# A dense layer with Mish on one core: the first block grows from 256 to 512 rows, half of it loaded by a DMA transpose that goes third on its queue

## The chip, the core and the metric

The kernel runs on one core of a Trainium2 chip. A core has a matrix engine (TensorE, PE in the profile, whose weight loads are shown as PEld), a vector engine (DVE), a scalar engine (ACT), GpSimd (POOL) and a queue engine (SP) that here only issues transfers. The engines run by themselves and meet at semaphores. Matrix products land in PSUM, eight banks of 128 partitions by 512 float32 values; everything else lies in SBUF, with 128 partitions too. The metric is the device time of one execution in microseconds.

## The reference

```python
def reference(x, w1, b1, w2):
    h = jnp.einsum("bsd,df->bsf", x, w1) + b1
    sp = jnp.log1p(jnp.exp(-jnp.abs(h))) + jnp.where(h > 0, h, jnp.zeros_like(h))
    act = h * jnp.tanh(sp)
    return jnp.einsum("bsf,fd->bsd", act, w2)
```

All tensors are bfloat16: x is 1 x 2048 x 512, w1 is 512 x 1792, b1 has 1792 values, w2 is 1792 x 512. So there are two matrix products with the Mish function between them.

## The kernel before

The 2048 rows of x are cut into blocks of 256, 512, 512, 512 and 256 rows (`BLOCKS`), and a block into tiles of 128 rows. For each block the kernel first computes the hidden layer, 14 slices `f` of 128 hidden units: `mm1_step` multiplies one 128 x 128 piece of w1 (slice f, one of four pieces k of the inner dimension) with the block's rows of x, which must lie transposed in `xT`, so four matmuls as wide as the block make one slice in one PSUM bank. ACT then adds b1 and applies Mish in one instruction per slice (`mish`), from PSUM into `a_sb`. After the 14 slices, `mm2` computes the output: for each tile of 128 rows, 14 matmuls of 512 columns accumulate over f in one bank, DVE copies the bank to `o_sb`, and SP stores it (`put`). The last tile is cut into 384 and 128 columns so that its second store is small.

The order is the order in which the code is written; there is no scheduler. Each engine waits only where `wait` puts a semaphore, and a `Stream` leaves out waits that an earlier one already covers.

The start is special. x must be transposed before it can be multiplied. For the first block, SP loads its two tiles as they are (`x_nat`), PE transposes them through PSUM in eight 128 x 128 transposes (`transpose_x`), and DVE and ACT copy one half of each tile to `xT`. For all later blocks SP issues DMA transposes that write `xT` straight from memory. SP issues in this order: tiles 0 and 1 of x, w1 for slices 4 to 7 (512 KB), w1 for slices 8 to 13 (768 KB), w2 for slices 0 to 4 (640 KB), w2 for slices 5 to 13 (1152 KB), and then the four DMA transposes. ACT issues w1 for slices 0 to 3 in two halves of 256 KB (k = 0, 1 and k = 2, 3), and b1. While the first transfers are under way, PE runs six matmuls of 512 columns on constants (`WARM`, `dummy`) that nobody reads. The first block's slices 0 to 3 are multiplied tile by tile as the copies land, and its second product runs f by f over both tiles at once, so that each piece of w2 is used as it lands. b1 arrives as 14 rows and is turned into a column per slice by one more PE transpose and a DVE copy (`b1_sb`).

Of the kernel before, what the change touches and what calls it, by code (L numbers as in the profile page):

```python
# [4 lines left out]

P = 128
WARM = (512,) * 6
BLOCKS = (256, 512, 512, 512, 256)


class Stream:
# [20 lines left out]
def bass_standalone__dense_activation_mish__prompt_kernel(  # L32
# [20 lines left out]
    F0 = 4  # L53
    N0 = BLOCKS[0] // P

    with ExitStack() as es:
        def sb(name, shape, t):
            return es.enter_context(nc.sbuf_tensor(name, shape, t))

        x_nat = sb("x_nat", [P, N0, D], BF)  # L60
# [4 lines left out]
        b1_pad = sb("b1_pad", [P, P], BF)  # L65
# [10 lines left out]
        sp = Stream(nc.sync, None)  # L76
        pe = Stream(nc.tensor, sem("c_pe"))
# [4 lines left out]
        def load(q, dst, src, name, transpose=False):  # L82
            s = sem(name)
            (q.eng.dma_start_transpose if transpose else q.eng.dma_start)(dst, src).then_inc(s, 16)  # L84
            return (s, 16)

        def load_w1(q, ks, a, b):
            return load(q, w1_sb[:, ks, a * P:b * P], w1v[:, ks, a * P:b * P], "s_w1_%d_%d" % (ks.start, a))


        t_xn, t_w1, t_w2 = [None] * N0, {}, {}
        for ks in (slice(0, 2), slice(2, 4)):
            t = load_w1(act, ks, 0, F0)
            for f in range(F0):
                for k in range(ks.start, ks.stop):
                    t_w1[k, f] = t
        for j in range(N0):
            t_xn[j] = load(sp, x_nat[:, j, :], x2[j * P:(j + 1) * P, :], "s_xn%d" % j)
        t_b1 = load(act, b1_nat[:, :], b1.rearrange("(j p) -> j p", p=P), "s_b1")
        for a, b in ((4, 8), (8, FT)):  # L100
            t = load_w1(sp, slice(0, KT), a, b)
            for f in range(a, b):
                for k in range(KT):
                    t_w1[k, f] = t
        for a, b in ((0, 5), (5, FT)):
# [3 lines left out]
        t_xT = [None]  # L109
# [15 lines left out]
        def dummy(n):  # L125
            nc.tensor.matmul(ps[:, 7, 0:n], c_w, c_m[:, 0:n], start=True, stop=True)  # L126


        free = [[] for _ in range(8)]
        t_cp = {}  # L130
        t_mish = {}

        def transpose_x(j):

            pe.wait(t_xn[j], t_id)
            for h, eng in ((0, dve), (1, act)):
                bank = 2 * j + h
                psb = ps[:, bank, 0:P].bitcast(BF)
                for i in range(2):
                    k = 2 * h + i  # L140
                    mm = nc.tensor.transpose(psb[:, i * P:(i + 1) * P], x_nat[:, j, k * P:(k + 1) * P], ident[:, :])  # L141
                eng.wait(pe.mark(mm))
                dst = xT[:, 2 * h:2 * h + 2, j * P:(j + 1) * P]
                src = psb.rearrange("p (k t) -> p k t", k=2)
                t = eng.mark(nc.vector.tensor_copy(dst, src) if eng is dve else act.eng.activation(dst, src, ACT.Copy))  # L145
                t_cp[j, h] = t
                free[bank] = [t]

        def mish(s, f, bank, t_mm):
            n = BLOCKS[s]  # L150
            act.wait(t_b1c, t_mm)
            t = act.mark(act.eng.activation(a_sb[:, f, starts[s]:starts[s + 1]], ps[:, bank, 0:n], ACT.Mish,  # L152
                                            bias=b1_sb[:, f:f + 1]))
            t_mish[s, f] = t
            free[bank] = [t]

        def mm1_step(s, f, k, bank, js=None):

            n = BLOCKS[s]
            lo, hi = (0, n) if js is None else (js[0] * P, (js[-1] + 1) * P)  # L160
            first = k == 0 and lo == 0
            if first:
                pe.wait(*free[bank])
            pe.wait(t_w1[k, f])
            if s:
                pe.wait(t_xT[s])
            else:
                pe.wait(*[t_cp[j, k // 2] for j in (js or range(N0))])
            return nc.tensor.matmul(ps[:, bank, lo:hi], w1_sb[:, k, f * P:(f + 1) * P],  # L169
                                    xT[:, k, starts[s] + lo:starts[s] + hi], start=first, stop=(k == KT - 1))  # L170

        def mm1(s, f, bank):
            for k in range(KT):
                mm = mm1_step(s, f, k, bank)
            mish(s, f, bank, pe.mark(mm))

        s_out = sem("s_out")
        n_out = 0

        def mm2_step(i, f, lo, hi, bank):  # L180
            s = max(b for b in range(len(BLOCKS)) if starts[b] <= i * P)
            if f == 0:
                pe.wait(*free[bank])
            pe.wait(t_w2[f], t_mish[s, f])
            return nc.tensor.matmul(ps[:, bank, 0:hi - lo], a_sb[:, f, i * P:(i + 1) * P], w2_sb[:, f, lo:hi],  # L185
                                    start=(f == 0), stop=(f == FT - 1))

        def put(i, lo, hi, bank, t_mm):
            nonlocal n_out
            dve.wait(t_mm)  # L190
            t = dve.mark(nc.vector.tensor_copy(o_sb[:, i, lo:hi], ps[:, bank, 0:hi - lo]))  # L191
            free[bank] = [t]
            sp.wait(t)
            sp.eng.dma_start(out2[i * P:(i + 1) * P, lo:hi], o_sb[:, i, lo:hi]).then_inc(s_out, 16)
            n_out += 1

        def mm2(i, lo, hi, bank):
            for f in range(FT):
                mm = mm2_step(i, f, lo, hi, bank)
            put(i, lo, hi, bank, pe.mark(mm))  # L200
# [7 lines left out]
        t_b1p = dve.mark(nc.vector.tensor_copy(b1_pad[0:FT, :], b1_nat[:, :]))  # L208
        done = []
        for js, ks in (((0,), (0, 1)), ((1,), (0, 1)), ((0, 1), (2, 3))):  # L210
            for k in ks:
                for f in range(F0):
                    mm = mm1_step(0, f, k, 4 + f, js)
                    if k == KT - 1:
                        done.append((f, 4 + f, pe.mark(mm)))
        for k in range(KT):
            mm = mm1_step(0, F0, k, 1)
        done.append((F0, 1, pe.mark(mm)))
        pe.wait(t_b1p, *free[0])
        psb1 = ps[:, 0, 0:P // 2].bitcast(BF)  # L220
        t_b1t = pe.mark(nc.tensor.transpose(psb1, b1_pad[:, :], ident[:, :]))  # L221
        dve.wait(t_b1t)
        t_b1c = dve.mark(nc.vector.tensor_copy(b1_sb[:, :], psb1[:, 0:FT]))  # L223
        free[0] = [t_b1c]
        for f, bank, t in done:
            mish(0, f, bank, t)
        for f in range(F0 + 1, FT):
            mm1(0, f, {5: 2, 6: 3, 7: 0, 12: 2, 13: 3}.get(f, 4 + f % 4))
        for f in range(FT):
            for j in range(N0):  # L230
                mm = mm2_step(j, f, 0, D, j)
                if f == FT - 1:
                    put(j, 0, D, j, pe.mark(mm))

        for s in range(1, len(BLOCKS)):
            for f in range(FT):
                mm1(s, f, 4 + f % 4)
# [35 lines left out]
```

## Time and profile before

| what | value |
|---|---|
| median of 3 runs | 106.25 us (106.18 to 106.25) |
| the profiled execution's own time: its span, first to last instruction | 105.4 us |
| PE busy | 101.1 us (96%), 532 matmuls recorded |
| PE weight loads busy | 52.0 us |
| ACT busy | 42.3 us |
| DVE busy | 12.2 us |
| DMA moved | 7.94 MB |
| granted TensorE clock, mean | 1.000 |

The runs' median is 0.85 us above the profiled span, since a run's time also holds what lies around the first and the last instruction. A busy PE in such a table is not a PE at its best pace, since matmuls overlap and are recorded from entering to leaving: two kernels are compared by when each stage starts, not by busy time.

### The profile page before, as it was taken

What the parts mean: (1) busy time and instruction counts of PE and PEld (TensorE: products, weight loads), DVE (VectorE), ACT (ScalarE), POOL (GpSimd) and SP (SyncE); (2) the same over time, 40 slices, a digit from 0 to 9 for tenths busy, and PEclk for the clock granted to TensorE, in tenths of its full rate; (3) what the DMA queues carried; (4) which work ended last, traced back from release to release, by engine and by line L of the source; (5) the groups of instructions that cost most, each with busy time, mean ns of one, the idle gap of its engine ahead of it and who ended that gap; (6) DMA issues with size and microseconds to landing.
All of it is one profiled execution on the core that took longest, in us unless ns stands there. A gap on an engine that the chain in (4) does not pass through costs nothing.

```text
span 105.4 us, 1227 instructions
## 1 busy us (share of the span) xinstructions
PE 101.1 (96%) x532; PEld 52.0 (49%) x541; DVE 12.2 (12%) x22; ACT 42.3 (40%) x73; POOL 0.7 (1%) x6
## 2 busy tenths in 40 slices
PE   6889999999999999999999999999999999999992
PEld 2477734444444444444444444444444444688462
DVE  0200000400001122200000222200000222200023
ACT  0607910477770000277771000177772000199100
POOL 2000000000000000000000000000000000000000
DMA  1999999980000111000000110110000101110011
GB/s 45 361 364 358 346 207 146 255 214 0 0 0 0 50 53 53 24 25 0 3 0 0 50 50 14 42 50 0 0 0 0 49 5 45 50 56 0 0 50 50
DMA packets 13489, 7.94 MB, mean 75 GB/s; under 512 B 7852, under 2 KB 13484, under 8 KB 13484
## 3 DMA queue, kind: packets, MB, share of 16 engines
q1 hardware_dynamic: 12912, 7.34, 26.3%
q10 hardware_dynamic: 572, 0.53, 1.5%
q8 instruction: 4, 0.07, 0.3%
q14 instruction: 1, 0.01, 0.0%
HBM read 3.94 MB, written 2.10 MB: 57 GB/s over the span
## 4 chain that ended last, share of the span: by engine, by line
PE 84%; DMA 11%; SPq 2%; issue 1%; DVE 0%
PE ps L185 44%; PE ps L169 40%; DMA w_sb<-in_w_dram 11%; SPq L84 2%; DVE o_sb L191 0%
## 5 line engine op out<-in xcount | busy, mean ns | idle before, releaser
L152 ACT ACTIVATE a_sb<-ps,b_sb 128x512 bf16<-128x512 f32 (+1 forms) x70 | 40.2, 611 | 52.2 <-PE ps L169 49.3
L169 PE MATMUL ps<-xT,w_sb 128*128 128x512 bf16 (+2 forms) x285 | 50.0, 334 | 0.7 <-DMA w_sb<-in_w_dram 0.3
L185 PE MATMUL ps<-w_sb,a_sb 128*128 128x512 bf16 (+2 forms) x232 | 48.7, 366 | 0.4
L169 PEld LDWEIGHTS ps<-xT,w_sb 128*128 128x128 bf16 x288 | 27.8, 100 | 22.2 <-DMA w_sb<-in_w_dram 0.6
L185 PEld LDWEIGHTS ps<-w_sb,a_sb 128*128 128x128 bf16 x238 | 22.7, 98 | 25.8 <-DMA w_sb<-in_w_dram 0.6
L191 DVE CAST o_sb<-ps 128x512 bf16<-128x512 f32 (+2 forms) x17 | 11.1, 660 | 84.3 <-PE ps L185 84.3
L126 PE MATMUL ps<-const-bfloat16-1.0 128*128 128x512 bf16 x6 | 2.7, 623 | 0.8 <-PEq L258 0.8
L120 ACT ACT_TABLE_LOAD x1 | 1.3, 1283 | 2.5 <-issue 2.5
L126 PEld LDWEIGHTS ps<-const-bfloat16-1.0 128*128 128x128 bf16 x6 | 0.7, 133 | 1.9 <-issue 1.9
L141 PE MATMUL ps<-ident,x_nat 128*128 128x128 bf16 x8 | 1.2, 309 | 0.4 <-DMA x_nat<-in_x_dram 0.4
L141 PEld LDWEIGHTS ps<-ident,x_nat 128*128 128x128 bf16 x8 | 0.7, 134 | 1.4 <-DMA x_nat<-in_x_dram 1.4
L145 ACT ACTIVATE xT<-ps 128x256 bf16<-128x256 bf16 x2 | 0.8, 384 | 0.9 <-PE ps L141 0.9
L145 DVE COPY xT<-ps 128x256 bf16<-128x256 bf16 x2 | 0.6, 292 | 3.6 <-PE ps L141 3.6
L208 DVE COPY b_pad<-b_nat 14x128 bf16<-14x128 bf16 x1 | 0.2, 182 | 1.6 <-DMA b_nat<-in_b_dram 1.6
L223 DVE CAST b_sb<-ps 128x14 f32<-128x14 bf16 x1 | 0.2, 174 | 1.3 <-PE ps L221 1.3
L118 POOL TENSOR_SCALAR_AFFINE_SELECT ident<-ones 128x128 bf16<-128x128 bf16 x1 | 0.3, 294 | 0.1
L221 PE MATMUL ps<-ident,b_pad 128*128 128x128 bf16 x1 | 0.2, 219 | 0.0
L115 DVE MEMSET b_pad<- 128x64 uint32 x1 | 0.1, 112 | 0.9 <-PEq L258 0.9
L116 POOL MEMSET ones<- 128x128 bf16 x1 | 0.2, 205 | 0.3 <-POOLq L258 0.3
L221 PEld LDWEIGHTS ps<-ident,b_pad 128*128 128x128 bf16 x1 | 0.1, 98 | 0.0
L258 POOL MEMSET const-bfloat16-1.0<- 128x1 bf16 x1 | 0.1, 102 | 0.0
L258 POOL MEMSET const-uint8-127<- 128x1 uint8 x1 | 0.1, 102 | 0.0
(2 smaller groups left out, 0.2 us busy)
## 6 DMA issues: line engine op xcount, KB each, us to landing
out_dram<-o_sb SPq DMA_DIRECT2D x15, 128.0 KB, 1.7
w_sb<-in_w_dram SPq DMA_DIRECT2D x1, 1152.0 KB, 11.4
w_sb<-in_w_dram SPq DMA_DIRECT2D x1, 768.0 KB, 7.4
w_sb<-in_w_dram SPq DMA_DIRECT2D x1, 640.0 KB, 8.7
w_sb<-in_w_dram ACTq DMA_DIRECT2D x2, 256.0 KB, 3.5
w_sb<-in_w_dram SPq DMA_DIRECT2D x1, 512.0 KB, 5.8
x_nat<-in_x_dram SPq DMA_DIRECT2D x2, 128.0 KB, 2.8
out_dram<-o_sb SPq DMA_DIRECT2D x1, 96.0 KB, 1.6
```

The lines of the kernel that those rows point to most:

```text
L84: (q.eng.dma_start_transpose if transpose else q.eng.dma_start)(dst, src).then_inc(s, 16)
L116: t_ones = pool.mark(pool.eng.memset(ones[:, :], 1.0))
L118: t_id = pool.mark(pool.eng.affine_select(ident[:, :], ones[:, :], pattern=[[1, P]], compare_op=ALU.is_equal, fill=0.0, base=0, channel_mu ...
L120: act.eng.preload_act_table(ACT.Mish)
L126: nc.tensor.matmul(ps[:, 7, 0:n], c_w, c_m[:, 0:n], start=True, stop=True)
L141: mm = nc.tensor.transpose(psb[:, i * P:(i + 1) * P], x_nat[:, j, k * P:(k + 1) * P], ident[:, :])
L145: t = eng.mark(nc.vector.tensor_copy(dst, src) if eng is dve else act.eng.activation(dst, src, ACT.Copy))
L152: t = act.mark(act.eng.activation(a_sb[:, f, starts[s]:starts[s + 1]], ps[:, bank, 0:n], ACT.Mish, bias=b1_sb[:, f:f + 1]))
L169: return nc.tensor.matmul(ps[:, bank, lo:hi], w1_sb[:, k, f * P:(f + 1) * P], xT[:, k, starts[s] + lo:starts[s] + hi], start=first, stop=( ...
L185: return nc.tensor.matmul(ps[:, bank, 0:hi - lo], a_sb[:, f, i * P:(i + 1) * P], w2_sb[:, f, lo:hi], start=(f == 0), stop=(f == FT - 1))
L191: t = dve.mark(nc.vector.tensor_copy(o_sb[:, i, lo:hi], ps[:, bank, 0:hi - lo]))
L221: t_b1t = pe.mark(nc.tensor.transpose(psb1, b1_pad[:, :], ident[:, :]))
```

## The change

`BLOCKS` becomes four blocks of 512, so the first block now has tiles 0 to 3. Tiles 0 and 1 are loaded and transposed on PE as before. Tiles 2 and 3 come by a DMA transpose of 256 rows, which SP issues third, behind tiles 0 and 1 of x and ahead of all of w1 and w2 that SP loads. The other three DMA transposes, of 512 rows each, stay behind w2.

On PE the constants' matmuls are now five of 512 columns and three of 128, and two more of 128 columns stand behind the transposes of tile 0. Slices 0 to 3 are multiplied in this order: tile 0 with k = 0, the transposes of tile 1, tile 0 with k = 1, tile 1 with k = 0 and 1, both tiles with k = 2 and 3 (256 columns), and then tiles 2 and 3 slice by slice (256 columns). From slice 4 on every matmul of the first product has 512 columns. The second product of the first block runs tile by tile, as in the other blocks.

DVE alone copies the transposed x tiles (128, 384, 256 and 256 columns), and b1 is turned by four 32 x 32 transposes on DVE in place of the one on PE. The store of the last 128 columns is issued by ACT and no longer by SP.

```diff
-WARM = (512,) * 6
-BLOCKS = (256, 512, 512, 512, 256)
+WARM = (512,) * 5 + (128,) * 3
+GAP = (128,) * 2
+FIRST = ((0, 2), (2, 4))
+BLOCKS = (512, 512, 512, 512)
...
+        for ks in FIRST:
+            load_w1(act, slice(*ks), 0, F0)
+        load_x(0)
+        load_x(1)
+        t_b1 = load(act, b1_nat[:, :], b1.rearrange("(j p) -> j p", p=P), "s_b1")
+        load_xT(2 * P, 4 * P)
+        load_w1(sp, slice(0, KT), 4, 8)
+        load_w1(sp, slice(0, KT), 8, FT)
+        load_w2(0, 5)
+        load_w2(5, FT)
         for s in range(1, len(BLOCKS)):
-            lo, hi = starts[s], starts[s + 1]
-            t_xT.append(load(sp, xT[:, :, lo:hi], x2[lo:hi, :], "s_xT%d" % s, True))
+            load_xT(starts[s], starts[s + 1])
...
         for n in WARM:
             dummy(n)
-        transpose_x(0)
-        transpose_x(1)
+        transpose_x(0, 6, (0,))
+        transpose_x(0, 5, (1, 2, 3))
+        for n in GAP:
+            dummy(n)
+        for k in range(2):
+            for f in range(F0):
+                mm1_step(0, f, k, f, 0, 1)
+            if k == 0:
+                transpose_x(1, 6, (0, 1))
+                transpose_x(1, 4, (2, 3))
         dve.wait(t_b1, t_bz)
         t_b1p = dve.mark(nc.vector.tensor_copy(b1_pad[0:FT, :], b1_nat[:, :]))
...
+        for c in range(P // 32):
+            t_b1t = dve.mark(nc.vector.transpose(b1_t[c * 32:(c + 1) * 32, :], b1_pad[:, c * 32:(c + 1) * 32]))
...
+        for k in range(2):
+            for f in range(F0):
+                mm1_step(0, f, k, f, 1, 2)
+        for k in range(2, KT):
+            for f in range(F0):
+                mm1_step(0, f, k, f, 0, 2)
+        for f in range(F0):
+            for k in range(KT):
+                mm = mm1_step(0, f, k, f, 2, 4)
+            mish(0, f, f, pe.mark(mm))
...
-                    mm2(i, D - P, D, (i + 1) % 4)
+                    mm2(i, D - P, D, (i + 1) % 4, act)
```

The order of instructions on PE from the start to the end of the first block, before. L126 is the matmuls on constants, L141 the transposes of x, L169 the first product, L221 the transpose of b1, L185 the second product:

```order
L126 MATMUL ps<-const-bfloat16-1.0 128x512 x6
L141 MATMUL ps<-ident,x_nat 128x128 x8
L169 MATMUL ps<-xT,w_sb 128x128 x16
L169 MATMUL ps<-xT,w_sb 128x256 x12
L221 MATMUL ps<-ident,b_pad 128x128
L169 MATMUL ps<-xT,w_sb 128x256 x36
L185 MATMUL ps<-w_sb,a_sb 128x512 x28
```

The same stretch of PE after the change, where L134 is the constants, L145 the transposes, L163 the first and L191 the second product:

```order
L134 MATMUL ps<-const-bfloat16-1.0 128x512 x5
L134 MATMUL ps<-const-bfloat16-1.0 128x128 x3
L145 MATMUL ps<-ident,x_nat 128x128 x4
L134 MATMUL ps<-const-bfloat16-1.0 128x128 x2
L163 MATMUL ps<-xT,w_sb 128x128 x4
L145 MATMUL ps<-ident,x_nat 128x128 x4
L163 MATMUL ps<-xT,w_sb 128x128 x12
L163 MATMUL ps<-xT,w_sb 128x256 x24
L163 MATMUL ps<-xT,w_sb 128x512 x40
L191 MATMUL ps<-w_sb,a_sb 128x512 x56
```

Four multiplications of tile 0 moved ahead of the transposes of tile 1, and the block's narrow matmuls (256 columns) went from 48 to 24, with 40 of 512 columns behind them.

SP's loads before, in the order of issue (x_nat are tiles 0 and 1, the four w_sb rows are w1 for slices 4 to 7 and 8 to 13 and w2 for 0 to 4 and 5 to 13):

```order
L84 DMA x_nat<-in_x_dram 128x512 x2
L84 DMA w_sb<-in_w_dram 128x4x512
L84 DMA w_sb<-in_w_dram 128x4x768
L84 DMA w_sb<-in_w_dram 128x5x512
L84 DMA w_sb<-in_w_dram 128x9x512
L84 DMA_TRANSPOSE xT<-in_x_dram 128x4x512 x3
L84 DMA_TRANSPOSE xT<-in_x_dram 128x4x256
```

SP's loads after the change:

```order
L86 DMA x_nat<-in_x_dram 128x512 x2
L86 DMA_TRANSPOSE xT<-in_x_dram 128x4x256
L86 DMA w_sb<-in_w_dram 128x4x512
L86 DMA w_sb<-in_w_dram 128x4x768
L86 DMA w_sb<-in_w_dram 128x5x512
L86 DMA w_sb<-in_w_dram 128x9x512
L86 DMA_TRANSPOSE xT<-in_x_dram 128x4x512 x3
```

The DMA transpose of 256 rows moved from the end of the row of loads to its third place, ahead of four copies of weights.

More of the change, by code (lines that the diff above doesn't have):

```diff
@@ L58, in sb @@
             return es.enter_context(nc.sbuf_tensor(name, shape, t))
-        x_nat = sb("x_nat", [P, N0, D], BF)
+        x_nat = sb("x_nat", [P, 2, D], BF)
         xT = sb("xT", [P, KT, S], BF)
@@ L64, in bass_standalone__dense_activation_mish__prompt_kernel @@
         b1_nat = sb("b1_nat", [FT, P], BF)
[L65 removed]
+        b1_pad = sb("b1_pad", [32, P], BF)
+        b1_t = sb("b1_t", [P, 32], BF)
         b1_sb = sb("b1_sb", [P, FT], F32)
@@ L85, in load, with load_x, load_w2 @@
             return (s, 16)
+        t_xn, t_w1, t_w2, t_xT = [None] * 2, {}, {}, {}
+        def load_x(j):
+            t_xn[j] = load(sp, x_nat[:, j, :], x2[j * P:(j + 1) * P, :], "s_xn%d" % j)
         def load_w1(q, ks, a, b):
[L88 to L94, printed above, removed]
+            t = load(q, w1_sb[:, ks, a * P:b * P], w1v[:, ks, a * P:b * P], "s_w1_%d_%d" % (ks.start, a))
+            for f in range(a, b):
                 for k in range(ks.start, ks.stop):
                     t_w1[k, f] = t
[L97 to L105, printed above, removed]
+        def load_w2(a, b):
             t = load(sp, w2_sb[:, a:b, :], w2v[:, a:b, :], "s_w2_%d" % a)
@@ L131, in bass_standalone__dense_activation_mish__prompt_kernel, with transpose_x @@
         t_mish = {}
[L133 to L147, printed above, removed]
+        def transpose_x(j, bank, ks):
+            pe.wait(t_xn[j], t_id, *free[bank])
+            psb = ps[:, bank, 0:2 * P].bitcast(BF)
+            for i, k in enumerate(ks):
+                mm = nc.tensor.transpose(psb[:, i * P:(i + 1) * P], x_nat[:, j, k * P:(k + 1) * P], ident[:, :])
+            n = len(ks)
+            dve.wait(pe.mark(mm))
+            t = dve.mark(nc.vector.tensor_copy(xT[:, ks[0]:ks[0] + n, j * P:(j + 1) * P],
+                                               psb[:, 0:n * P].rearrange("p (k t) -> p k t", k=n)))
+            for k in ks:
+                t_cp[j, k] = t
+            free[bank] = [t]
@@ new lines, in mm1_step @@
+        def mm1_step(s, f, k, bank, j0=0, j1=None):
+            j1 = BLOCKS[s] // P if j1 is None else j1
+            lo, hi = j0 * P, j1 * P
+            first = k == 0 and j0 == 0
+            if first:
+                pe.wait(*free[bank])
+            pe.wait(t_w1[k, f])
+            for j in range(starts[s] // P + j0, starts[s] // P + j1):
+                pe.wait(t_cp[j, k] if j < 2 else t_xT[j])
+            return nc.tensor.matmul(ps[:, bank, lo:hi], w1_sb[:, k, f * P:(f + 1) * P],
+                                    xT[:, k, starts[s] + lo:starts[s] + hi], start=first,
+                                    stop=(k == KT - 1 and hi == BLOCKS[s]))
@@ L149, in mish @@
         def mish(s, f, bank, t_mm):
-            n = BLOCKS[s]
             act.wait(t_b1c, t_mm)
-            t = act.mark(act.eng.activation(a_sb[:, f, starts[s]:starts[s + 1]], ps[:, bank, 0:n], ACT.Mish,
+            t = act.mark(act.eng.activation(a_sb[:, f, starts[s]:starts[s + 1]], ps[:, bank, 0:BLOCKS[s]], ACT.Mish,
                                             bias=b1_sb[:, f:f + 1]))
@@ L155, in mish, with put @@
             free[bank] = [t]
[L157 to L175, printed above, removed]
         s_out = sem("s_out")
         n_out = 0
[L180 to L188, printed above, removed]
+        def put(i, lo, hi, bank, t_mm, q):
             nonlocal n_out
@@ L192, in put, with mm2 @@
             free[bank] = [t]
-            sp.wait(t)
-            sp.eng.dma_start(out2[i * P:(i + 1) * P, lo:hi], o_sb[:, i, lo:hi]).then_inc(s_out, 16)
+            q.wait(t)
+            q.eng.dma_start(out2[i * P:(i + 1) * P, lo:hi], o_sb[:, i, lo:hi]).then_inc(s_out, 16)
             n_out += 1
-        def mm2(i, lo, hi, bank):
+        def mm2(i, lo, hi, bank, q=sp):
+            s = max(b for b in range(len(BLOCKS)) if starts[b] <= i * P)
+            pe.wait(*free[bank])
             for f in range(FT):
-                mm = mm2_step(i, f, lo, hi, bank)
-            put(i, lo, hi, bank, pe.mark(mm))
+                pe.wait(t_w2[f], t_mish[s, f])
+                mm = nc.tensor.matmul(ps[:, bank, 0:hi - lo], a_sb[:, f, i * P:(i + 1) * P], w2_sb[:, f, lo:hi],
+                                      start=(f == 0), stop=(f == FT - 1))
+            put(i, lo, hi, bank, pe.mark(mm), q)
@@ L210, in bass_standalone__dense_activation_mish__prompt_kernel @@
[L210 to L221, printed above, removed]
@@ L222, in bass_standalone__dense_activation_mish__prompt_kernel @@
-        dve.wait(t_b1t)
[L223 to L237, printed above, removed]
+        dve.wait(t_b1p)
@@ L238, in bass_standalone__dense_activation_mish__prompt_kernel @@
+        for s in range(len(BLOCKS)):
+            for f in range(F0 if s == 0 else 0, FT):
+                for k in range(KT):
+                    mm = mm1_step(s, f, k, 4 + f % 4)
+                mish(s, f, 4 + f % 4, pe.mark(mm))
             for i in range(starts[s] // P, starts[s + 1] // P):
```

8 lines of the change are left out of this document (5 added, 3 removed).

## The prediction

> **What bounds the kernel now.** I read the page's busy shares first, then the chain of waits, and then the timeline of PE to see the pace of each stage.
>
> ```profile
> PE 101.1 (96%) x532; PEld 52.0 (49%) x541; DVE 12.2 (12%) x22; ACT 42.3 (40%) x73; POOL 0.7 (1%) x6
> PE ps L185 44%; PE ps L169 40%; DMA w_sb<-in_w_dram 11%; SPq L84 2%; DVE o_sb L191 0%
> 18.64 12.25 PE L169 MATMUL ps<-xT,w_sb 128*128 128x512 bf16 x55
> 30.73 12.25 PE L185 MATMUL ps<-w_sb,a_sb 128*128 128x512 bf16 x55
> 91.16 6.28 PE L169 MATMUL ps<-xT,w_sb 128*128 128x256 bf16 x56
> 97.49 6.03 PE L185 MATMUL ps<-w_sb,a_sb 128*128 128x512 bf16 x41
> ```
>
> The first two are from the page, the others from the timeline of PE: start, length, line, tiles, number recorded. PE never rests from 18.64 us on: 56 matmuls of 512 columns start every 12.09 us (30.73 - 18.64), 0.2159 us each; 56 of 256 columns take 97.49 - 91.16 = 6.33 us, 0.1130 us each, 5% more per column. A block of 512 rows costs (91.16 - 18.64) / 3 = 24.17 us, and PE ends at 97.49 + 6.03 = 103.52 us. Nothing can be won there but the 5%. All the rest must come from ahead of 18.64 us, where the chain holds a DMA of weights with 11%. The transfers of that stretch, with issue start and length from the timeline, and size and time from issue to landing from the list of issues by window:
>
> ```profile
> 1.26 0.41 SPq L84 DMA_DIRECT2D x_nat<-in_x_dram  x1
> x_nat<-in_x_dram SPq DMA_DIRECT2D x1, 128.0 KB, 3.1
> 0.80 0.98 ACTq L84 DMA_DIRECT2D w_sb<-in_w_dram  x2
> w_sb<-in_w_dram ACTq DMA_DIRECT2D x1, 256.0 KB, 3.2
> w_sb<-in_w_dram ACTq DMA_DIRECT2D x1, 256.0 KB, 3.8
> 1.72 2.27 SPq L84 DMA_DIRECT2D w_sb<-in_w_dram  x4
> w_sb<-in_w_dram SPq DMA_DIRECT2D x1, 512.0 KB, 5.8
> w_sb<-in_w_dram SPq DMA_DIRECT2D x1, 768.0 KB, 7.4
> w_sb<-in_w_dram SPq DMA_DIRECT2D x1, 1152.0 KB, 11.4
> 7.52 0.28 PE L169 MATMUL ps<-xT,w_sb 128*128 128x256 bf16 x1 [0.32 <-DMA w_sb<-in_w_dram]
> 9.72 0.27 PE L169 MATMUL ps<-xT,w_sb 128*128 128x256 bf16 x1 [0.23 <-ACT a_sb L152]
> 14.74 0.33 PEld L185 LDWEIGHTS ps<-w_sb,a_sb 128*128 128x128 bf16 x3 [0.58 <-DMA w_sb<-in_w_dram]
> ```
>
> Tile 1 of x lands at 1.26 + 3.1 = 4.4 us, the first half of w1 for slices 0 to 3 at 4.0, the second half, issued about 1.3, at 5.1, and w1 for slices 4 to 7 at 1.72 + 5.8 = 7.5, which is when PE starts again (7.52). The 768 KB land near 9.6 (issue about 2.2 + 7.4); PE waits until 9.72, and the ACT that the row names is not the cause. The last w2, 3.3 + 11.4, lands at 14.7, and the weight loads wait for it until 14.74. So three times in a row PE catches up with a weight transfer. A block of 256 rows has too little work per byte of weights; the loads set its pace.
>
> **What a larger first block does.** With 512 rows each slice keeps PE busy for 4 x 0.2159 = 0.86 us rather than 0.45, so weights that land as they do now come early, but for the first few. It adds a DMA transpose ahead of the weights. The four that exist now show its price, first the issues on SP, then the landings of the first, second and last, then the bandwidth (the last column, GB/s):
>
> ```profile
> 4.04 10.45 SPq L84 DMA_TRANSPOSE xT<-in_x_dram  x1
> 14.54 2.84 SPq L84 DMA_TRANSPOSE xT<-in_x_dram  x1
> 17.42 2.29 SPq L84 DMA_TRANSPOSE xT<-in_x_dram  x1
> 19.75 1.31 SPq L84 DMA_TRANSPOSE xT<-in_x_dram  x1
> xT<-in_x_dram SPq DMA_TRANSPOSE x1, 14.0
> xT<-in_x_dram SPq DMA_TRANSPOSE x1, 5.4
> xT<-in_x_dram SPq DMA_TRANSPOSE x1, 3.4
> 3.50:4.00 0.50, 0.48 (x5) 0.21 (x3) 0.19 (x1) 0.33 (x1) 0.00 (x0) 1.00 1.10 383
> 14.00:14.50 0.50, 0.50 (x4) 0.10 (x1) 0.00 (x0) 0.00 (x0) 0.00 (x0) 1.00 0.21 26
> 15.00:15.50 0.50, 0.50 (x4) 0.26 (x3) 0.00 (x0) 0.00 (x0) 0.00 (x0) 1.00 1.28 291
> ```
>
> The one of 256 rows (the last) holds SP for 1.31 us and lands 3.4 us after its issue; those of 512 rows hold it for 2.29 and 2.84. The first held SP for 10.45 us, with four weight copies ahead of it on the queue, and data came only from its end on: 26 GB/s just before 14.5 us, 291 after. While they move, transposes reach 291 GB/s where copies reach 383.
>
> New transpose: 262 KB at 291 GB/s is 0.90 us of the transfer engines. Its issue, 1.72 to 3.03 us, delays the issue of w1 by 1.31 us, but 786 KB of x and w1 are then still on their way (at the row's 383 GB/s, 2.1 us), so I take the delay of the weights as between 0.90 (transfer alone) and 1.31 (the whole issue) and put it at 1.0, near the transfer, since the engines have work throughout. w1 for slices 4 to 7 then lands at 8.5 us (8.4 to 8.8), the next part at 10.6, the last w2 at 15.7. The transpose itself lands at the earliest at 1.72 + 3.4 = 5.1; with 5.4, the time of the second one, at 7.1. I take 6.4: it moves alongside the copies ahead of it, and those alone end by 5.1.
>
> The Trainium skill ("DMA: Bandwidth & Descriptors", section Latency and other measured facts) gives 261 GB/s for DMA transposes with a strided middle dimension; by that the transfer would take an estimated 1.0 us and not 0.90, and the sum below would not change. The row above reads higher, 291.
>
> **The start on PE.** The rows needed:
>
> ```profile
> 1.22 0.15 PEld L126 LDWEIGHTS ps<-const-bfloat16-1.0 128*128 128x128 bf16 x1 [0.28 <-issue]
> 1.65 0.15 PEld L126 LDWEIGHTS ps<-const-bfloat16-1.0 128*128 128x128 bf16 x1 [0.28 <-issue]
> 3.35 0.63 PE L141 MATMUL ps<-ident,x_nat 128*128 128x128 bf16 x4
> L169 PE MATMUL ps<-xT,w_sb x9: 264/314/314, 4.8 to 5.7; 128*128 128x128 bf16 x9
> L169 PE MATMUL ps<-xT,w_sb x13: 219/220/314, 5.5 to 6.4; 128*128 128x128 bf16 x10, 128*128 128x256 bf16 x3
> 5.83 0.72 PE L169 MATMUL ps<-xT,w_sb 128*128 128x128 bf16 x8
> ```
>
> At first PE runs slow: constants every 0.43 us (1.65 - 1.22), twice 0.2159, and transposes, of 0.31 us each, every (0.63 - 0.31) / 3 = 0.107 us. The matmuls of 128 columns last 314 ns until about 5.6 us and 220 ns after it (minimum/median/maximum in the two rows), and then follow each other every (0.72 - 0.22) / 7 = 0.07 us. I keep that change of pace at 5.6 us. New order: constants from 0.84 us, 5 x 0.43 + 3 x 0.107 = 2.47, to 3.31; transposes of tile 0 from 3.35 to 3.78, two fillers to 3.99; w1 is there at 4.0, the DVE copy of 128 columns a little earlier, so four matmuls of tile 0 run from 4.03 to 4.46, over the wait for tile 1 (4.4) that PE now spends idle. Transposes of tile 1 to 4.89, four matmuls to 5.31; of the next eight, three slow to 5.63 and five quick to 5.98; eight of 256 columns (0.90) to 6.88. Tiles 2 and 3 are needed then and have landed at 6.4: sixteen of 256 columns, 1.81 us, to 8.69. w1 for slices 4 to 7 landed at 8.5. Then 40 of 512 columns, 8.63 us, to 17.32 us (the next w1, needed at 12.1, is there from 10.6). The second product takes 12.09 us, and w2 is long there; three blocks of 24.17 us end at 17.32 + 12.09 + 72.52 = 101.93 us, with the split last tile inside the last block as it is now inside 6.03. Against 103.52 that is 1.59 us less.
>
> Side work costs nothing while its cover holds. Mish starts when b1 is a column:
>
> ```profile
> 6.72 0.18 DVE L208 COPY b_pad<-b_nat 14x128 bf16<-14x128 bf16 x1 [1.57 <-DMA b_nat<-in_b_dram]
> L152 ACT ACTIVATE a_sb<-ps,b_sb 128x512 bf16<-128x512 f32 x42 | 28.9, 688 | 37.4 <-PE ps L169 37.4
> ```
>
> b1 is copied at 6.72, four small DVE transposes and a cast, at the copy's 0.18 each, bring it to 7.8 (no row shows such a transpose; at the 0.29 of the cast of 128 columns, below, to 8.4), ACT needs 0.69 us per slice against 0.86 on PE, and slice 4's bank has to be free when PE comes to slice 8. That holds if Mish starts by 8.7 us, 0.9 of slack; each us beyond it would be late on PE. The PE transpose of b1 that goes away was 0.1 of PE's work. The DVE copies in place of ACT's halves lie beside the matmuls of the other tile. The block's transposes on the later queue are wanted at 29 us instead of 18.64 and lose their tightness. The fillers end before x lands; without x they would cost 0.02.
>
> The last store:
>
> ```profile
> 103.55 0.29 DVE L191 CAST o_sb<-ps 128x128 bf16<-128x128 f32 x1 [0.22 <-PE ps L185]
> 103.36 0.33 SPq L194 DMA_DIRECT2D out_dram<-o_sb  x1
> 103.87 0.33 SPq L194 DMA_DIRECT2D out_dram<-o_sb  x1
> ```
>
> SP is free at 103.69, before the cast ends at 103.84, so moving the last store gains nothing; ACT's issues of loads took 0.49 (half of 0.98) against SP's 0.41, so I add 0.05 (0 to 0.1). Sum: 105.4 - 1.59 + 0.05 = 103.86 us of span. With the 0.85 us by which the median stands above the span, 104.7 us.
>
> **Rivals.** *The transpose is held until the copies ahead of it are through, and the gain is smaller.* For: the first transpose above moved nothing for about 0.5 us after the copies had ended. Against: the third was issued in 2.29 us while the first (landed 14 us after 4.04, at 18.0) and the second (19.9) were both under way, so two transfers ahead hold nothing. If SP holds it until tile 1 has landed at 4.4, its issue ends at 5.7; it moves until 6.7 and lands 1.1 later, as the first did, at 7.8. PE waits 0.9; w1, issued at 5.7 behind it, lands near 9.7, so slice 4 starts 1.0 late: 105.7 us. Held for less, down to nothing, it is between 104.7 and that.
>
> *The pace of PE changes later.* Each us by which the quick pace comes after 5.6 costs PE half a us. From 3.2 us later on, at 8.8, the 1.59 us are gone: 106.25, no change. Against it: before, PE idled 0.44 us between the two tiles' transposes (3.98 to 4.42) and was quick at 5.6 all the same; now it has less idling. And the three runs lie within 0.07 us, so the moment doesn't wander from run to run. The Trainium skill ("TensorE: Matmul & The Clock Gate", Part 1) says that the clock is released by a window of about 3.4 us of activity that runs freely, so that the moment depends on where the first matmul falls in it; by that, the change could come one window late, and the estimate would be 1.7 us lost, slightly slower than no change. The runs' spread of 0.07 us doesn't agree with a phase that falls anywhere.
>
> *Slower: the transpose is held as the first one was.* That one took 14.0 us from issue to landing, 7.9 of SP's 10.45 above the normal 2.57. Tiles 2 and 3 would land at 1.72 + 14.0 = 15.7 us, 8.8 after PE wants them, with w1 behind: 113.5 us. It decides from 8.47 us on (6.88 + 1.59, a landing 6.75 us after issue). For it: nothing in the trace says what held the first. Against: it had 3072 KB of copies ahead on its queue, the new one 256 KB, and three of four landed in 5.4 or less.
>
> **The numbers.** The forecast with its own range of 104.2 to 105.0 has 0.60; a smaller gain, 105.0 to 105.9, has 0.20; no change (within 0.2%, about what a measurement of this kernel can tell, 106.04 to 106.46) has 0.07; slower has 0.13. The low end is a w1 landing 0.3 early with PE's pace changing sooner, the high end is the first rival's 105.7 with 0.1 on top; together they leave out 0.2. Faster: 0.80.
>
> **What the profile after would show.** The transpose's issue near 1.72 us for about 1.3 us and its landing by 6.9; PE's first 512-column matmul at 8.7, the second product of block 0 at 17.3, no wait for w2, PE's end at 101.9. Wrong would be: a PE wait for xT or for w1 ahead of slice 4 of more than 0.3 us, 314 ns matmuls beyond 6 us, or PE waiting for ACT at slices 8 to 11 because b1 came late.

## The result and the profile after

| kernel | median us | lowest to highest | runs |
|---|---|---|---|
| before | 106.22 | 106.04 to 106.97 | 14 |
| changed | 105.27 | 104.83 to 106.46 | 14 |

The ratio is 0.9905 with a 95% interval of 0.9882 to 0.9927, so the change saves 0.95 us by the medians. 104.7 had been forecast, in a range of 104.2 to 105.8; 105.27 lies in the part of it, 105.0 to 105.9, that had been given a chance of 0.20, and not in the forecast's own 104.2 to 105.0. In every execution of either kernel whose span is on record, the time stands 1.2 to 1.35 us above its own span, 1.26 in the middle. The first profile of the changed kernel is of its slowest execution, 106.46 us. Ratios leave out the few executions that lie over 1.5% above the fastest of their kernel, this one among them, while the medians count all. A second profile was taken, of 105.88 us. Both are used below: the first for what can go wrong in a single late execution, the second for the rest.

The first profile, from the page: span, PE, the chain by line, and the bandwidth in 40 slices of 2.63 us:

```profile
span 105.2 us, 1142 instructions
PE 101.3 (96%) x495; PEld 48.9 (47%) x504; DVE 13.6 (13%) x28; ACT 39.3 (37%) x57; POOL 0.7 (1%) x6
PE ps L191 46%; PE ps L163 44%; DMA xT<-in_x_dram 6%; SPq L86 1%; DVE o_sb L180 0%
GB/s 40 319 109 361 355 349 275 170 229 44 50 50 50 0 0 6 0 0 50 50 50 50 0 0 0 3 6 50 50 50 50 0 0 0 0 0 53 53 50 50
```

The DMA in the chain was w2 before (11%); now it is the transposing load of tiles 2 and 3 (6%). Its issue and the loads behind it, then the landings of that load, of w1 for slices 4 to 7 and of the last w2, and PE where it waits:

```profile
1.72 1.31 SPq L86 DMA_TRANSPOSE xT<-in_x_dram  x1
3.08 3.70 SPq L86 DMA_DIRECT2D w_sb<-in_w_dram  x4
xT<-in_x_dram SPq DMA_TRANSPOSE x1, 6.3
w_sb<-in_w_dram SPq DMA_DIRECT2D x1, 512.0 KB, 6.4
w_sb<-in_w_dram SPq DMA_DIRECT2D x1, 1152.0 KB, 11.9
8.10 2.57 PE L163 MATMUL ps<-xT,w_sb 128*128 128x256 bf16 x18 [0.64 <-DMA xT<-in_x_dram]
18.49 0.38 PE L191 MATMUL ps<-w_sb,a_sb 128*128 128x512 bf16 x1
94.68 8.62 PE L191 MATMUL ps<-w_sb,a_sb 128*128 128x512 bf16 x52
```

SP is held for 1.31 us, as the nearest row of before said. The load lands at 1.72 + 6.3 = 8.0 us and PE waits 0.64 us for it. The weights land at 9.5 (3.08 + 6.4) and, issued at 5.14, at 17.0, and no longer hold anybody. The second product starts at 18.49 and PE ends at 94.68 + 8.62 = 103.30, 0.2 before the 103.52 of the old profile.

In the second profile the same rows read:

```profile
xT<-in_x_dram SPq DMA_TRANSPOSE x1, 4.8
w_sb<-in_w_dram SPq DMA_DIRECT2D x1, 512.0 KB, 5.1
4.93 0.61 PE L145 MATMUL ps<-ident,x_nat 128*128 128x128 bf16 x4 [0.33 <-DMA x_nat<-in_x_dram]
17.91 1.46 PE L191 MATMUL ps<-w_sb,a_sb 128*128 128x512 bf16 x6
93.67 9.05 PE L191 MATMUL ps<-w_sb,a_sb 128*128 128x512 bf16 x55
```

Here tiles 2 and 3 land at 6.5 us and w1 at 8.2 (3.08 + 5.1), early enough, and PE waits only for tile 1. Still, its second product starts at 17.91, where 17.32 was forecast. From there to PE's end it is 84.81 us in both profiles (103.30 - 18.49 and 102.72 - 17.91), so each execution's time is fixed by when the second product of the first block starts. The forecast had 84.61 for that stretch, 0.2 too little.

### The profile page after: what moved, and what is told of

The parts are those of the page before. It is cut to its first block, busy times and chain, and to the rows that moved or that the text cites. A ratio compares the mean times of both kernels' runs of the same rounds, so it can differ in the third digit from the quotient of the medians.

```text
span 105.2 us, 1142 instructions
## 1 busy us (share of the span) xinstructions
PE 101.3 (96%) x495; PEld 48.9 (47%) x504; DVE 13.6 (13%) x28; ACT 39.3 (37%) x57; POOL 0.7 (1%) x6
## 4 chain that ended last, share of the span: by engine, by line
PE 90%; DMA 6%; SPq 1%; issue 1%; DVE 0%
PE ps L191 46%; PE ps L163 44%; DMA xT<-in_x_dram 6%; SPq L86 1%; DVE o_sb L180 0%
## 5 line engine op out<-in xcount | busy, mean ns | idle before, releaser
L169 ACT ACTIVATE a_sb<-ps,b_sb 128x512 bf16<-128x512 f32 x56 | 38.0, 688 | 50.0 <-PE ps L163 50.0
L163 PE MATMUL ps<-xT,w_sb 128*128 128x512 bf16 (+2 forms) x243 | 50.1, 365 | 0.9 <-DMA xT<-in_x_dram 0.6
L191 PE MATMUL ps<-w_sb,a_sb 128*128 128x512 bf16 (+2 forms) x234 | 48.8, 366 | 0.2
L163 PEld LDWEIGHTS ps<-xT,w_sb 128*128 128x128 bf16 x248 | 24.3, 101 | 25.7 <-DMA xT<-in_x_dram 0.9
L191 PEld LDWEIGHTS ps<-w_sb,a_sb 128*128 128x128 bf16 x238 | 22.8, 98 | 25.9
L134 PE MATMUL ps<-const-bfloat16-1.0 128*128 128x512 bf16 (+1 forms) x10 | 3.0, 467 | 0.8 <-PEq L251 0.8
L134 PEld LDWEIGHTS ps<-const-bfloat16-1.0 128*128 128x128 bf16 x10 | 1.2, 139 | 2.2 <-issue 2.2
L148 DVE COPY xT<-ps 128x256 bf16<-128x256 bf16 (+2 forms) x4 | 1.1, 291 | 3.5 <-PE ps L145 3.4
L145 PE MATMUL ps<-ident,x_nat 128*128 128x128 bf16 x8 | 1.2, 310 | 0.0
L145 PEld LDWEIGHTS ps<-ident,x_nat 128*128 128x128 bf16 x8 | 0.7, 133 | 0.4 <-DMA x_nat<-in_x_dram 0.3
L212 DVE STREAM_TRANSPOSE b_t<-b_pad 32x32 bf16<-32x32 bf16 x4 | 0.8, 202 | 0.1
L126 POOL TENSOR_SCALAR_AFFINE_SELECT ident<-ones 128x128 bf16<-128x128 bf16 x1 | 0.3, 295 | 0.1
```

The source lines that it names most:

```text
L126: t_id = pool.mark(pool.eng.affine_select(ident[:, :], ones[:, :], pattern=[[1, P]], compare_op=ALU.is_equal, fill=0.0, base=0, channel_mu ...
L148: t = dve.mark(nc.vector.tensor_copy(xT[:, ks[0]:ks[0] + n, j * P:(j + 1) * P], psb[:, 0:n * P].rearrange("p (k t) -> p k t", k=n)))
L191: mm = nc.tensor.matmul(ps[:, bank, 0:hi - lo], a_sb[:, f, i * P:(i + 1) * P], w2_sb[:, f, lo:hi], start=(f == 0), stop=(f == FT - 1))
L212: t_b1t = dve.mark(nc.vector.transpose(b1_t[c * 32:(c + 1) * 32, :], b1_pad[:, c * 32:(c + 1) * 32]))
```

## The experiments

Theory 1 says that what lands when, the transposing load above all, sets the start of the second product and its spread. Theory 2 says that it is the moment at which PE goes over to its quick pace. Ratios are to the kernel before on the same chip.

| kernel | median us | ratio (95%) | PE quick from, in its profile | second product starts | span |
|---|---|---|---|---|---|
| changed, again | 105.31 | 0.9905 (0.9867 to 0.9942) | 6.65 | 17.91 | 104.6 |
| no load of tiles 2, 3 | 105.15 | 0.9898 (0.9868 to 0.9928) | 5.75 | 17.33 | 104.1 |
| tiles 2, 3 by PE | 106.21 | 0.9979 (0.9952 to 1.0006) | 3.6 | 17.7 | 104.5 |
| that load on ACT's queue | 111.65 | 1.047 (1.0424 to 1.0516) | 6.3 | 24.8 | 111.5 |
| same, SP held meanwhile | 106.96 | 1.0038 (1.0000 to 1.0076) | 4.75 | 18.92 | 105.6 |
| old blocks, the rest changed | 106.42 | 0.9969 (0.9934 to 1.0005) | 6.4 | 12.2 | 105.3 |
| no constants | 106.37 | 0.9970 (0.9929 to 1.0011) | 7.75 | 18.25 | 105.0 |
| old constants, no fillers | 105.44 | 0.9896 (0.9840 to 0.9951) | 6.3 | 17.58 | 104.3 |
| tile 1 transposed first, as before | 105.27 | 0.9880 (0.9827 to 0.9933) | 3.8 to 4.5 | 16.93 | 103.6 |
| that load twice | 106.23 | 0.9968 (0.9937 to 0.9998) | 4.8 | 18.13 | 104.8 |

The moment of the quick pace is where the weight loads, in a row, go from 0.15 us to 0.10 (the first one after a wait is 0.10 at any pace). "Second product" is that of the first block, of 256 rows with the old blocks.

**The changed kernel again**, unchanged:

> The changed kernel once more, for a second profile and more times. In the first one tiles 2 and 3 landed at 8.05 us (6.4 was forecast), PE waited 0.64 us for them, the quick pace came at about 6.3 us (5.6 was forecast) and slice 4 started at 10.0 us (8.7). Theory 1 (the transpose's landing sets the time, and varies): a run near 105.0 us shows a landing before 7.5 us; the wait for tiles 2 and 3 goes with the time. Theory 2 (the moment of PE's quick pace varies): the landing stays near 8.0 and the matmuls of 314 ns end at another time, 5.6 us or earlier in a run near 104.9.

Neither theory alone explains it. This execution, half a us above the median, had its tiles 2 and 3 at 6.5 us and no wait for them, so its lateness is not theory 1's. Its weight loads say where it comes from; then the same of the kernel with the old constants, and of the one without any:

```profile
6.40 0.26 PEld L163 LDWEIGHTS ps<-xT,w_sb 128*128 128x128 bf16 x2
6.77 0.10 PEld L163 LDWEIGHTS ps<-xT,w_sb 128*128 128x128 bf16 x1
```

```profile
6.06 0.25 PEld L163 LDWEIGHTS ps<-xT,w_sb 128*128 128x128 bf16 x2
6.37 0.10 PEld L163 LDWEIGHTS ps<-xT,w_sb 128*128 128x128 bf16 x1
17.58 1.67 PE L191 MATMUL ps<-w_sb,a_sb 128*128 128x512 bf16 x7
```

```profile
7.52 0.15 PEld L163 LDWEIGHTS ps<-xT,w_sb 128*128 128x128 bf16 x1
7.87 0.10 PEld L163 LDWEIGHTS ps<-xT,w_sb 128*128 128x128 bf16 x1
18.25 1.03 PE L191 MATMUL ps<-w_sb,a_sb 128*128 128x512 bf16 x4
```

Two loads that take 0.26 us together and overlap by some 0.04 are still slow ones, two that take 0.15 together are quick ones, and so is one of 0.10 in a full row. Quick at 6.3 starts the second product at 17.58, quick at 7.75 at 18.25: 0.67 us for 1.45, about half a us per us.

**Without the load of tiles 2 and 3:**

```diff
-        load_xT(2 * P, 4 * P)
...
+        for j, t in ((0, t_cp[0, 3]), (1, t_cp[1, 3])):
+            dve.wait(t)
+            t = dve.mark(nc.vector.tensor_copy(xT[:, :, (j + 2) * P:(j + 3) * P], xT[:, :, j * P:(j + 1) * P]))
```

> The transposing load of tiles 2 and 3 is left out; DVE copies the columns of tiles 0 and 1 into their place (so rows 256 to 511 of the result repeat rows 0 to 255), and everything else stays. Theory 1: no wait for tiles 2 and 3, w1 for slices 4 to 7 lands near 7.5 us rather than 9.5, slice 4 starts at 8.7 to 9.3 us; the median falls to 104.6 and the runs lie within 0.4 us. Theory 2: the start stays as slow as PE's pace makes it; the median falls by 0.2 at most, to 105.1, and the runs spread over 0.8 us or more as they do with the load.

The medians differ by 0.16 us (105.15 against 105.31), and the lowest runs are equal, 104.88 and 104.83. The spread is smaller, 0.75 us against 1.07 here, but not gone. So the load, though it delays the weights by more than a us, costs almost nothing of the median. Whether it adds late executions like the first profile, six runs do not show. In this kernel's profile w1 for slices 4 to 7 lands at 6.8:

```profile
w_sb<-in_w_dram SPq DMA_DIRECT2D x1, 512.0 KB, 5.1
5.51 0.25 PEld L162 LDWEIGHTS ps<-xT,w_sb 128*128 128x128 bf16 x2
5.80 0.15 PEld L162 LDWEIGHTS ps<-xT,w_sb 128*128 128x128 bf16 x2
17.33 1.89 PE L190 MATMUL ps<-w_sb,a_sb 128*128 128x512 bf16 x8
```

The second product nevertheless starts only at 17.33: PE itself is the limit there, quick from 5.75.

**Tiles 2 and 3 by PE**, as tiles 0 and 1:

```diff
-        load_xT(2 * P, 4 * P)
+        load_x(2)
+        load_x(3)
...
+        transpose_x(2, 5, (0, 1))
+        transpose_x(2, 7, (2, 3))
         for k in range(2, KT):
             for f in range(F0):
                 mm1_step(0, f, k, f, 0, 2)
+        transpose_x(3, 6, (0, 1))
+        transpose_x(3, 4, (2, 3))
```

> Tiles 2 and 3 come as tiles 0 and 1 do: two plain loads of 128 KB in the third and fourth place of SP's queue, eight more transposes on PE, four more copies on DVE; no DMA transpose ahead of w1. Theory 1: two plain loads take 0.7 us of the transfer engines and not 2, w1 for slices 4 to 7 lands near 8.2 us; PE has 8 x 0.06 to 0.11 = 0.5 to 0.9 us more to do and no wait: 105.0 to 105.4. Theory 2: PE's work is what counts, so 0.5 to 0.9 slower than the change: 105.8 to 106.2.

106.21, by the ratios 0.8 us above the change, is at the upper end of theory 2's numbers. It is not PE's work alone: the profile, of an execution with a very early quick pace (3.6), shows PE waiting 0.36 us for DVE, on the copies of tile 3:

```profile
7.37 3.42 PE L164 MATMUL ps<-xT,w_sb 128*128 128x256 bf16 x23 [0.36 <-DVE xT L149]
```

**The load on ACT's queue**, third behind two halves of w1:

```diff
+        load_xT(2 * P, 4 * P, act)
         t_b1 = load(act, b1_nat[:, :], b1.rearrange("(j p) -> j p", p=P), "s_b1")
-        load_xT(2 * P, 4 * P)
...
+        sp.wait(t_xT[2])
         for s in range(1, len(BLOCKS)):
```

> The transpose of tiles 2 and 3 goes third on ACT's queue, behind the two halves of w1 and ahead of b1, and SP issues w1 for slices 4 to 7 right behind tiles 0 and 1; SP's later transposes wait for the first one. If the transfer engines stall around a transpose whatever queue it is on (theory 1): the low bandwidth of about 1.5 us comes again, tiles 2 and 3 land at 8 us or later, the median is 105.0 to 105.8. If only the place in SP's queue and the 1.31 us of its issue cost time: w1 for slices 4 to 7 lands at 8.0 to 8.5, tiles 2 and 3 near 7, and the median is 104.7 or less. Theory 2: 105.2, like the change.

All the times expected were wrong: 111.65. Issue, landing, PE's wait, and three stretches, in the first two of which the copies of SP ran beside the transpose (the last column is GB/s, the third from the right the granted clock). The profile is of an execution of 112.78 us:

```profile
1.82 1.36 ACTq L86 DMA_TRANSPOSE xT<-in_x_dram  x1
xT<-in_x_dram ACTq DMA_TRANSPOSE x1, 10.5
12.42 1.89 PE L164 MATMUL ps<-xT,w_sb 128*128 128x256 bf16 x8 [5.02 <-DMA xT<-in_x_dram]
7.50:8.00 0.50, 0.00 (x0) 0.00 (x0) 0.00 (x0) 0.00 (x0) 0.00 (x0) 1.00 1.24 105
10.50:11.00 0.50, 0.00 (x0) 0.00 (x0) 0.00 (x0) 0.00 (x0) 0.00 (x0) 0.50 1.03 280
16.00:17.00 1.00, 1.00 (x5) 0.35 (x3) 0.00 (x0) 0.86 (x2) 0.00 (x0) 0.72 1.34 326
```

It landed 10.5 us after its issue, and all transfers together moved 105 GB/s from 7.5 to 8.0 us, while the transfer engines were busy. The late landing is not the whole loss. While PE waits, the granted clock falls to 0.50, and it comes back only between 16 and 17 us. From the landing to the second product it takes 24.8 - 12.4 = 12.4 us here, where the same work took 10.4 in the kernel with tile 1 first (below), so some 2 us were lost to the pace. The mean clock was below 0.99 in all six executions.

**The same with SP's weights held back** until it has landed:

```diff
+        sp.wait(t_xT[2])
         load_w1(sp, slice(0, KT), 4, 8)
```

> The kernel with the transpose third on ACT's queue (111.65 us; tiles 2 and 3 landed at 12.3 us there), with one more wait: SP issues w1 for slices 4 to 7 and all behind it only when that transpose has landed, so no copy from SP moves beside it but tiles 0 and 1. If the copies from the other queue were what slowed it: tiles 2 and 3 land at 6 to 7 us, w1 for slices 4 to 7 about 3 us after that, and the time is 106 to 107.5. If ACT's queue itself is slow for a transpose: they land after 10 us, and the time is 113 or more.

```profile
1.83 1.31 ACTq L86 DMA_TRANSPOSE xT<-in_x_dram  x1
xT<-in_x_dram ACTq DMA_TRANSPOSE x1, 4.4
10.28 8.81 PE L165 MATMUL ps<-xT,w_sb 128*128 128x512 bf16 x40 [1.68 <-DMA w_sb<-in_w_dram]
```

Landed 4.4 us after issue, with PE waiting for w1 instead, 106.96. So it was the copies of the other queue that held it, not ACT's queue. In the changed kernel the copies of SP stand behind the transpose on one queue, and it lands as early as here: 4.3 to 4.8 us after issue in every profile with it on SP's queue but the first.

**The load twice**, the second time into a spare place:

```diff
         load_xT(2 * P, 4 * P)
+        load(sp, xT_spare[:, :, :], x2[2 * P:4 * P, :], "s_spare", True)
```

> The changed kernel with the transposing load of tiles 2 and 3 issued twice, the second time into a place that nobody reads, third and fourth on SP's queue. By the forecast's price each takes 0.9 to 1.0 us of the transfer engines and 1.31 us of SP: w1 for slices 4 to 7 lands at 9.3 to 10.5 instead of 8.2 to 9.5, later than PE comes to it (8.9 to 9.3), so the time grows by 0.5 to 1.3 us, to 105.8 to 106.6. If the transposes' time on the queue is hidden however long: 105.3, within 0.2.

```profile
xT_spare<-in_x_dram SPq DMA_TRANSPOSE x1, 4.1
5.23 2.28 SPq L87 DMA_DIRECT2D w_sb<-in_w_dram  x4
w_sb<-in_w_dram SPq DMA_DIRECT2D x1, 512.0 KB, 4.2
9.49 8.81 PE L165 MATMUL ps<-xT,w_sb 128*128 128x512 bf16 x40 [0.95 <-DMA w_sb<-in_w_dram]
```

As expected: w1 lands at 9.4 us (5.23 + 4.2), 1.2 after the second profile's 8.2, and PE waits 0.95 for it. The median is 0.96 above that of the kernel with tile 1 first (below, 105.27), which ran on the same chip and does as well as the change; by the ratios it is 0.7 above the change. The first such load uses up the slack; most of a second one is paid.

**Old blocks with the rest of the change** (constants, fillers, tile 0 ahead of tile 1, the last store):

```diff
-WARM = (512,) * 6
+WARM = (512,) * 5 + (128,) * 3
+GAP = (128,) * 2
 BLOCKS = (256, 512, 512, 512, 256)
```

> The kernel before, with its blocks of 256, 512, 512, 512, 256 and its loads, and with three parts of the change: the constants' matmuls of other sizes and the two fillers, tile 0 with k = 0 ahead of the transposes of tile 1, and the last store on ACT. If the larger first block is what gains (theory 1): the weights still set the pace, PE waits for them at about 7.5, 9.6 and 14.7 us, and the time is 106.25, within 0.2. If the earlier start on PE is what gains: 105.8 or less.

0.9969 (0.9934 to 1.0005): nothing that can be told from no change. PE's waits in its profile, and the start of the second block:

```profile
9.61 2.78 PE L170 MATMUL ps<-xT,w_sb 128*128 128x256 bf16 x24 [0.32 <-DMA w_sb<-in_w_dram]
14.61 3.57 PEld L186 LDWEIGHTS ps<-w_sb,a_sb 128*128 128x128 bf16 x18 [0.56 <-DMA w_sb<-in_w_dram]
18.51 1.67 PE L170 MATMUL ps<-xT,w_sb 128*128 128x512 bf16 x7
```

PE still waits for w1 and for the last w2. So most of the gain comes with the larger first block; the DVE copies and b1 on DVE, which came with it, were not undone by themselves.

**The constants.** The changed kernel without any (`WARM = ()`, `GAP = ()`), and with the six of before and no fillers (`WARM = (512,) * 6`, `GAP = ()`):

> The changed kernel without any matmul on constants; PE starts with the transposes of tile 0 at about 3.4 us. Theory 2 (the quick pace comes after some stretch of PE's own activity, at a moment that falls differently in each run): it comes later by up to 2.5 us, each us costs half a us, 105.8 to 106.6, and the 314 ns matmuls go on beyond 6.5 us. Theory 1 (only landings count): 105.3 as with them, within 0.2, since w1 for slices 4 to 7 lands at 8.2 to 9.5 anyhow.

> The changed kernel with the six constants' matmuls of 512 columns of the kernel before, and no fillers behind the transposes of tile 0. If filling the gaps brings the quick pace sooner: it comes later without them, 105.6 or more. If the moment does not hang on gaps of 0.2 us (theory 2's free phase, and theory 1): 105.3, within 0.2.

Without constants 0.9970, close to 0.7 us worse than the change's ratio and 0.8 worse than the kernel with the old constants on the same chip. Its profile shows theory 2's mechanism, a quick pace from 7.75 only. With the old ones 0.9896, as with the new: the fillers and the other sizes do nothing that shows.

**Tile 1 transposed ahead of tile 0's first products:**

```diff
+        transpose_x(1, 6, (0, 1))
+        transpose_x(1, 4, (2, 3))
         for k in range(2):
             for f in range(F0):
                 mm1_step(0, f, k, f, 0, 1)
-            if k == 0:
-                transpose_x(1, 6, (0, 1))
-                transpose_x(1, 4, (2, 3))
```

> The changed kernel with the transposes of tile 1 ahead of the first four multiplications of tile 0, as before the change. The forecast had those four cover PE's wait for tile 1, worth 4 x 0.107 = 0.43 us at PE's slow pace: the second product starts 0.4 later at the same moment of the quick pace, and the median is 105.6 to 105.8. If another limit hides it (tiles 2 and 3, or w1 for slices 4 to 7 at 8.2 to 9.5 us): 105.3, within 0.2.

No loss: 105.27. Its profile happens to be of a quick execution, 103.6 us of span, and shows what stops those:

```profile
6.54 0.22 PEld L163 LDWEIGHTS ps<-xT,w_sb 128*128 128x128 bf16 x3 [0.21 <-DMA xT<-in_x_dram]
16.93 2.32 PE L191 MATMUL ps<-w_sb,a_sb 128*128 128x512 bf16 x10
```

PE was quick by 4.5 us and ready for tiles 2 and 3 before they landed, at 6.5. From that landing it takes 1.81 + 8.63 us to the second product: 16.94, and 16.93 is measured. 103.6 us of span is also that of the fastest runs of the changed kernel (104.83). So theory 1's landing is the limit in this execution, as theory 2's moment was in the second profile. That the landing is the floor of every quick execution is not shown: the fastest run without the load has a span of 103.6 too.

**The kernel before again**, for a second profile:

> The kernel before once more, for a second profile. The forecast set out from a profiled span of 105.4 us and put the median 0.85 us above it; in all other runs the time stands 1.26 us above the span, so that first profile belongs to an execution of about 106.65, 0.4 above the median. Theory 1 (before, the weights' landings set the time): a span near 105.0 us shows the last w2 landing about 0.4 us before 14.7 and the second block starting as much before 18.64, whatever the moment of the quick pace. Theory 2 (the moment of PE's quick pace): the landing is where it was, and the matmuls of 314 ns end before 5.6 us.

Theory 1, on both counts. Its time is 106.26, its span 105.0; the last w2, the start of the second block, and the quick pace:

```profile
w_sb<-in_w_dram SPq DMA_DIRECT2D x1, 1152.0 KB, 11.0
18.28 1.46 PE L169 MATMUL ps<-xT,w_sb 128*128 128x512 bf16 x6
5.63 0.18 PEld L169 LDWEIGHTS ps<-xT,w_sb 128*128 128x128 bf16 x2
9.29 2.78 PE L169 MATMUL ps<-xT,w_sb 128*128 128x256 bf16 x24 [0.30 <-DMA w_sb<-in_w_dram]
```

w2 landed 0.4 us sooner after its issue than the 11.4 of the first profile, the second block starts at 18.28 instead of 18.64, and the quick pace is at the same 5.6 us. With the old blocks and the rest changed, the quick pace came at 6.4 us, but the last w2 landed at 14.6, between the two others, and the second block started at 18.51, between them too. In all three profiles 3.9 us lie between this landing and that start, whatever PE's pace was before.

## Why the prediction came out as it did

*The mechanism was right.* Before, the landing of the last w2 set the end of the first block: 3.9 us lie from it to the second block in three profiles. Without the larger block almost nothing is gained (0.9969). The waits for weights are gone in the second profile of the change. One of the three waits that the prediction counted was of that execution alone: in the second profile of before, w1 for slices 4 to 7 lands at 6.8 and PE doesn't wait for it, only for the rest of w1 and for the last w2.

*The step that was off is the last one, from the profiled execution to the median.* The forecast took 0.85 us as what lies between them. It is 1.26, so the profiled execution of before must have been one of about 106.65, 0.4 above its median. The sum's 1.55 us was a gain over a late execution of the old kernel. With 1.26, the same sum gives 103.86 + 1.26 = 105.12, against 105.27. That is 0.42 of the missed 0.57 us; the remaining 0.15 is near the 0.2 by which 84.61 was too little.

*PE's start came out as counted, in part by luck, since its moment wanders.* The median of 105.27 is a span of 104.0, and with the 86.7 us from the second product to the end of the span (105.2 - 18.49) that is a start at 17.3; forecast was 17.32. No profile shows at what moment the median execution becomes quick, so this agreement is no proof of the count; its slope is better borne out. Moved by half a us per us from the quick pace at 5.6, it gives 17.67 at 6.3 (17.58 measured), 18.4 at 7.75 (18.25) and 17.85 at 6.65 (17.91). But the moment lay between 3.6 and 6.65 in the profiles of kernels with constants, and between 4.75 and 6.65 in those whose program for PE is the same as the change's. The argument against that, runs within 0.07 us, was wrong: in the kernel before, PE waits for the last w2 whatever its pace was, so its runs could not show it. Fourteen runs of it spread over 0.9 us anyhow. The Trainium skill ("TensorE: Matmul & The Clock Gate", Part 1) says that the window of activity runs freely and the same kernel becomes quick at a different point in each run; the profiles agree, with a spread of 1.9 us for one program of PE. The forecast had given that rule little weight. Of its own signs of being wrong, slow matmuls beyond 6 us stood in both profiles and a wait for xT of more than 0.3 us in the first.

*The transposing load.* Its 1.31 us on SP are as forecast. On SP's queue it landed at 6.0 to 6.6 us in five profiles, where 6.4 was taken, and at 8.0 in the first profile. Its price on the queue was set low: against the kernel without it, w1 lands 1.4 us later (8.2 against 6.8), above the 0.9 to 1.31 that had been bounded. The bandwidth shows the reason; the stretch from 4.5 to 6.5 us in the second profile and without the load, and a quarter of a us of the first profile:

```profile
4.50:6.50 2.00, 1.67 (x16) 1.57 (x16) 1.05 (x5) 0.00 (x0) 0.00 (x0) 1.00 1.21 232
4.50:6.50 2.00, 2.00 (x24) 1.93 (x22) 0.99 (x5) 0.00 (x0) 0.00 (x0) 1.00 1.09 356
5.75:6.00 0.25, 0.25 (x6) 0.25 (x4) 0.00 (x0) 0.00 (x0) 0.00 (x0) 1.00 1.96 26
```

While the load moves, all transfers together carry 232 GB/s instead of 356, some 250 KB less in 2 us. With the load's own 262 KB that is 1.4 us at 356 GB/s, an estimate from these rows. The price of 0.90 counted the load's own bytes only. The 26 GB/s, known from the prediction's row ahead of the first transpose of before, came back, with the load on SP's queue, in the first profile alone; why this execution had them is open. That w1 was forecast at 8.5 and landed at 8.2 all the same is luck: the 7.5 from which the forecast set out was the late landing of one execution (6.8 and 6.9 in the three other profiles without a transpose ahead of w1), 0.6 to 0.7 too high, while the price was 0.4 too low.

*Terms that came to nothing.* The four products ahead of tile 1 were in the sum with 0.43 us; undone, the median is the same. In an execution with an early quick pace PE waits for tiles 2 and 3 instead; why late ones show no loss either is not settled, since six runs with a spread of 1.15 us would hide some 0.3 (the upper end of the interval is 0.9933). The fillers did nothing, as counted. ACT's issue of the last store took 0.38 us against SP's 0.33, the 0.05 that was added. b1 was a column at 8.0 us in the first profile, after four DVE transposes of 0.20 each, and ACT had the slack.

*The rivals.* The held transpose (105.7) is what the first profile shows in part: a landing at 8.0 and PE waiting, but with SP free on time, so not for the reason given. The wandering pace was not a case by itself, but a part of every execution's time. The slow rival did not occur on SP's queue; on ACT's, with copies beside it, it did.

## What to carry to other kernels

Find out how far the profiled execution lies from the median (its time against its own span) before a sum is set against it. A wait for weights early in a kernel is removed by giving each weight more rows, and it pays until the next landing or PE itself is the limit; double the new transfer to see how much slack is left. Put a DMA transpose on the queue that carries the bulk copies, ahead of them: on the other queue, with those copies beside it, it took more than twice as long here.

## What the runs showed of the hardware

A DMA transpose of 256 rows landed 4.4 us after issue when only the early loads were beside it, 4.3 to 4.8 with copies queued behind it on SP's queue (6.3 in one late execution), and 10.5 with copies from the other queue, at 105 to 280 GB/s for everything together. The granted clock in the profile reads 1.00 in the first microseconds, while matmuls run at half their later pace. The traces hold no record of the clock for that time: the first one stands at 6.53 us in the first profile of the change and at 6.70 in the second, within some 0.2 us of the change of pace, and six of the thirteen traces have none. With PE idle from 7.4 us on, in the kernel with the load on ACT's queue, the column falls to 0.50 some 2.3 us later (10.5 to 11.0 us above). So a 1.00 there doesn't rule out the slow start; the length of the weight loads, 0.15 us against 0.10, shows it.
